# A first batch's weights: W1 fetched in fp32 and cast by ScalarE, with z and W2 moved in GpSimd's order

## The chip, the cores and the metric

The kernel runs on one core of a Trainium2 chip. A core has a matrix engine (TensorE, PE in the profile, with its weight loads as PEld), a vector engine (VectorE, DVE), an activation engine (ScalarE, ACT), GpSimd (POOL) and SyncE (SP), which here only issues DMAs. The engines share an on-chip memory, SBUF, of 128 partitions; TensorE writes into PSUM, from where DVE and ACT read. Engines run on their own and wait for each other by semaphores. DMAs are issued by SP, ACT or POOL and carried out by 16 DMA engines.

The metric is the device time of one execution in microseconds.

## What is computed

For each of 8 batches of 3008 rows: a gated attention without a softmax, and then a feed-forward layer with a quick gelu.

```python
scores = (1 / S) * z @ z.T                  # z: 3008 x 64, S = 3008
attn   = max(scores, 0) ** 2
x      = u * (attn @ v)                     # u, v: 3008 x 256
h      = x @ w_in                           # w_in (W1): 256 x 2048
out    = (h * sigmoid(1.702 * h)) @ w_out   # w_out (W2): 2048 x 256
```

Inputs and output are fp32. The kernel computes in fp16 with fp32 sums in PSUM.

## The kernel before

A batch's 3008 columns of the score matrix are cut into 6 chunks `i` of 512 (the last has 448), its rows into 24 blocks of 128. For chunk `i` the function `attend` gives a list of 47 steps `n` (slots 0 to 46): each multiplies blocks of V by the squared scores of one row block and adds into two PSUM banks. A place in the program is written (i, n) here.

Everything is in one order written out by hand (`manual_schedule`): each engine takes its instructions in the order in which the program names them. The main loop (lines 648 to 714) goes over batches, chunks and slots, and at each slot does in this order what the tables say: `turn_u` (a transpose of u by DVE), `load_u`, `load_w`, `load_z`, `take` (the next scores), an up group, and the step itself.

- `take` (line 613, tables `SCHED0` and others) issues scores ahead of their use. `scores` (line 223) writes a tile of two PSUM banks, of which there are two (`ps2`, `bufs=2`), shared with the up groups. `square` (line 242) lets ACT take the relu (line 256) and DVE square it (line 270). In chunk 3 of batch 0 scores are taken at slots 0, 4, 8, 12, 16, 19, 24 (two), 29, 33, 37, 41 and 45.
- Since the scores are symmetric, half of the squared tiles are gained by transposing others (`turn_unit`, line 293), as DMAs of SP (tiles `tt`).
- `up_group` (line 389) is the first feed-forward product: four matmuls with W1 into a `ps2` tile, the gelu by ACT (line 407), and a scaling to fp16 by DVE (line 411). Sixteen of a batch's 48 run between the steps of chunk 4, which is where W1 is first read. `product` (line 499) is the second, with W2 and four sums of W2's quarters (`weight_sums`, line 442, called in chunk 5), in Strassen's way with seven products.
- In chunks 2, 3 and 5 of batch 0 the steps run on halves of the array: `post` (line 84) puts a `pool.nop` (line 86) into POOL's order after step 23, which waits for the step's matmuls; the first matmul of step 24 waits for it (`behind`, line 91).
- POOL issues most loads: `load_u` (line 188, four DMAs), `load_w` (line 430) and `load_z` (line 152), with a dtype cast from fp32 to fp16 in W's and z's DMAs. `load_z` issues one half of the next batch's z, copies it on POOL once it has landed (line 162), hands it to SP to be transposed into `ZT` (line 163), and does the same with the other half. The two fp16 halves lie in tiles `zst` of tag `y` of the pool `pw`, which has two buffers. The same tag holds the first batch's z in fp32 (`zf`) at the start, and the output tiles `y` later.
- In the first batch the table `LOADW` (line 598) puts W1's four fourths at (3, 16), (3, 24), (3, 32), (3, 40) and W2's at (4, 16), (4, 22), (4, 28), (4, 34). Before the first of them POOL makes a small copy `hold` (line 434) that waits for chunk 1's gated result. `load_z` of the next batch stands at (4, 2) in every batch, and `load_u` of chunk 5 at (4, 8).

Of the kernel before, what the change touches and what calls it, by code (L numbers as in the profile page):

```python
# [9 lines left out]
F32 = mybir.dt.float32  # L10
F16 = mybir.dt.float16
P = 128
# [3 lines left out]
def kernel(  # L16
# [13 lines left out]
    AF = mybir.ActivationFunctionType  # L30
# [4 lines left out]
    DFF = moe_w_in.shape[1]  # L35
# [5 lines left out]
    NCH = (S + CH - 1) // CH  # L41
    CB = CH // P
    NU = NJ // 2
    NCC = D // P
# [11 lines left out]
    dve, act, pe, sp, pool = nc.vector, nc.scalar, nc.tensor, nc.sync, nc.gpsimd  # L56

    const = ctx.enter_context(tc.tile_pool(name="const", bufs=1))
    W1 = const.tile([P, NCC, DFF], F16, name="W1")
# [6 lines left out]
    pw = ctx.enter_context(tc.tile_pool(name="pw", bufs=2))  # L66
# [7 lines left out]
    nil = pw.tile([P, CH], F16, name="nil", tag="gf")  # L74
    dve.memset(nil, 0.0)

    ZP = {}
    late, LATE = [], []
    ZT, V16, UQ, UT, XT, unit, TT = {}, {}, {}, {}, {}, {}, {}

# [40 lines left out]
    def first_cast(g, by_act=False):  # L121
        m = g % CB * CB
        for c in range(2):
            dst, src = ZT["st"][g // CB][:, m:m + CB, c, :], ZT["f"][g // CB][:, m:m + CB, :]
            if by_act:
                act.activation(dst, src, AF.Copy, scale=1.0)  # L126
            else:
                dve.tensor_copy(dst, src)

    def first_zt(g):  # L130

        z2 = ZT["st"][g // CB][:, g % CB * CB:(g % CB + 1) * CB]
        zp = ZP[g] if g in ZP else ps1.tile([P, CB, P], F16, name="zp", tag="ps1")
        for k in range(CB):
            pe.transpose(zp[:, k, :], z2[:, k, :, :], ident)  # L135

        def copies():
            zt = ZT[0][:, g * CB:(g + 1) * CB, :].rearrange("d n p -> d (n p)")
            nb = CB if g < NCH - 1 else CB - 1
            dst = zt[:, :nb * P].rearrange("d (p n) -> d p n", n=nb)  # L140
            src = zp[:, :nb, :].rearrange("d n p -> d p n")
            if g in (0, 2, 3):
                act.activation(dst, src, AF.Copy, scale=1.0)  # L143
            else:
                dve.tensor_copy(dst, src)
            if nb < CB:
                dve.tensor_copy(zt[:, nb * P:], zp[:, nb, :])

        return copies
# [35 lines left out]
    def width(i):  # L185
        return CH if i < NCH - 1 else LAST

    def load_u(b, i):
        eng = pool if b or i else sp
        n = width(i)  # L190
        uq = pu.tile([P, CH // QW, QW, NCC], F32, name="uq", tag="uq")
        src = u[b, i * CH:i * CH + n].rearrange("(q t) c -> t q c", t=QW)
        for k in range(P // QW):
            cs = slice(k * NCC * QW, (k + 1) * NCC * QW)
            eng.dma_start(uq[k * QW:(k + 1) * QW, :n // QW].rearrange("t q c k -> t q (c k)"), src[:, :, cs])  # L195
        UQ[b, i] = uq

    def turn_u(b, i):
        n = width(i)
        ut = pu.tile([P, NCC, CH // QW, QW], F32, name="ut", tag="ut")  # L200
        UT[b, i] = ut
        dve.transpose(  # L202
            ut[:, :, :n // QW, :].rearrange("p k q t -> p q k t"),
            UQ.pop((b, i))[:, :n // QW].rearrange("p q c k -> p q k c"),
        )
# [114 lines left out]
    def full(b):  # L320

        return NCH - 2 if b < B - 1 else NCH - 1
# [107 lines left out]
    def load_w(k):  # L430

        if k == 0:
            hold = const.tile([P, 1], F16, name="hold")
            pool.tensor_copy(hold, XT[0, 1][:, 0, :1])
        if k < 4:
            fs = slice(k * DFF // 4, (k + 1) * DFF // 4)
            pool.dma_start(W1[:, :, fs], moe_w_in.rearrange("(p k) f -> p k f", k=NCC)[:, :, fs])
        else:
            fs = slice((k - 4) * CB, (k - 3) * CB)
            pool.dma_start(W2[:, fs], moe_w_out.rearrange("(fo p) c -> p fo c", p=P)[:, fs])  # L440

    def weight_sums():
        b11, b12, b21, b22 = W2[:, LO, C0], W2[:, LO, C1], W2[:, HI, C0], W2[:, HI, C1]
        t1, t2, t3, t4n = (WT[:, m] for m in range(4))
        return [
            lambda: dve.tensor_tensor(t1, b12, b11, ALU.subtract),  # L446
            lambda: dve.tensor_tensor(t2, b22, t1, ALU.subtract),  # L447
            lambda: dve.tensor_tensor(t3, b22, b12, ALU.subtract),
            lambda: dve.tensor_tensor(t4n, b21, t2, ALU.subtract),
        ]  # L450
# [27 lines left out]
    def products(b):  # L478

        lst = []  # L480
        for k in range(NCH):
            one = [(k, "P6"), (k, "P5"), (k, "P7"), (k, "P2")]
            if blocks(b)[k][1] < CH:
                one.insert(0, (k, "odd"))
            lst += [(k, "P1")] + ([(k - 1, "P4"), (k - 1, "P3")] if k else []) + one
        return lst + [(k, "P4"), (k, "P3")]
# [108 lines left out]
    TURN0 = {(i, (38, 28)[i] if i < 2 else NJ + 4 if i < NCH - 1 else 12): i for i in range(NCH)}  # L595
    LOAD0 = {(1, 14): 2, (2, 12): 3, (2, NJ + 20): 4, (4, 8): 5}
    TURN = {(1, NJ + 4): 2, (2, NJ + 4): 3, (4, NJ + 4): 4, (5, 8): 5}
    LOADW = {(3, 16): 0, (3, 24): 1, (3, 32): 2, (3, 40): 3, (4, 16): 4, (4, 22): 5, (4, 28): 6, (4, 34): 7}
    LOAD = {(3, NJ + 20): 4, (4, NJ + 5): 5}

    FIRST_ZT, FIRST_CAST = {12: 4, 20: 5}, {5: 4, 13: 5}
# [11 lines left out]
    def take(b, n):  # L613
        for post_ in scores(b, [queue.pop(0) for _ in range(n)]):
            post_()

    def fill(b):
        assert not queue
        queue.extend(u_ for i in range(NCH) for u_ in pieces(b, i))
# [24 lines left out]
    copies()  # L644
    ZP[3] = ps1.tile([P, CB, P], F16, name="zp", tag="ps1")
    load_u(0, 1)

    for b in range(B):
        nup = NCH * NFG
        more = b + 1 < B  # L650
        sched = SCHED0 if b == 0 else SCHED if more else SCHED_LAST
        turn, load = (TURN, LOAD) if b else (TURN0, LOAD0)
        head = 0
        for i in range(NCH):
            host = b + 1 if more and i == NCH - 1 else b
            if host > b:
                fill(host)
                LATE.append(host)
            for n, step in enumerate(attend(b, i, b == 0 and i < 2)):
                if b == 0 and i == 0 and n == 5:  # L660
                    load_u(0, 0)
                if b == 0 and i == 0 and n == 2:
                    copies = first_zt(3)
                if b == 0 and i == 0 and n == 3:
                    copies()
                if b == 0 and i == 0 and n in FIRST_CAST:
                    first_cast(FIRST_CAST[n], True)
                if b == 0 and i == 0 and n in FIRST_ZT:
                    first_zt(FIRST_ZT[n])()
                if (i, n) in turn:  # L670
                    turn_u(b, turn[i, n])
                if (i, n) in load:
                    load_u(b, load[i, n])
                if b == 0 and (i, n) in LOADW:
                    load_w(LOADW[i, n])
                if more and (i, n) == (NCH - 2, 2):
                    load_z(b + 1)
                if (b, i, n) == (0, NCH - 1, NJ + 4):
                    for sum_ in weight_sums():
                        sum_()  # L680
                take(host, sched[i].get(n, 0))
                if i == full(b) and n >= HEAD and (n - HEAD) * LAGY // (2 * NJ - 10) >= head and head < LAGY:
                    up_group(b, head)
                    head += 1
                step()
        late.sort(key=lambda t: t[0])
        if more:
            for i in range(2):
                load_u(b + 1, i)
            for n0 in range(0, NJ, VB):  # L690
                load_v(b + 1, n0)
        prods = products(b)
        for q in range(head, nup):
            if more and q in (head + 14, head + 20):
                k = int(q == head + 20)
                turn_u(b + 1, k)
                load_u(b + 1, k + 2)
            up_group(b, q)
            product(b, *prods.pop(0))
            if q >= 30 and q % 2 and late:  # L700
                late.pop(0)[1]()
        steps = [lambda kp=kp: product(b, *kp) for kp in prods]
        for step in steps:
            step()
            for sum_ in [SUMS.pop(0) for _ in range(min(len(SUMS), 1 + (len(SUMS) > 4)))]:
                sum_()
            for _, turn_it in [late.pop(0) for _ in range(min(len(late), 1 + (len(steps) < 10)))]:
                turn_it()
        LATE.clear()
        if more:  # L710
            while late:
                late.pop(0)[1]()
            take(b + 1, 2)
# [30 lines left out]
```

## Time and profile before

| what | value |
|---|---|
| median of 4 runs | 1185.6 us (1185.09 to 1190.59) |
| time of the profiled execution | 1185.6 us |
| its span, first to last instruction | 1183.8 us |
| TensorE busy | 1177.9 us |
| VectorE, ScalarE, GpSimd busy | 841.0, 819.8, 227.4 us |
| granted TensorE clock | 1.0 |
| first batch, to the first step of batch 1 | 161.3 us |
| batch 1, batch 2 | 147.1, 144.2 us |

The page lists each engine's busy time, the chain of work that ended last, and groups of instructions by line. A row of a group has the line, the engine, the operation, what it writes and reads, the count, the busy time, the mean time of one, and the idle time before it with what ended it. The timeline view gives, for one stretch, start, duration, engine, line and count of neighbouring instructions of the same kind, with the engine's idle time before them in brackets. A busy TensorE isn't one at its peak: matmuls overlap, so a hold-up of TensorE is better read from starts than from busy time.

### The profile page before, as it was taken

Reading aid. Unit: us, or ns where it says so; the run is one execution under the profiler, and the core shown is the slowest. Engines: PE = TensorE matmul, PEld = TensorE weight load, DVE = VectorE, ACT = ScalarE, POOL = GpSimd, SP = SyncE. Lnnn points to the kernel's source line nnn. Section 1 sums busy time; section 2 is a strip of 40 time slices with the busy share of each in tenths; the row PEclk is TensorE's granted clock in tenths of the full one; section 3 lists DMA queues with packets and bytes.
Section 4 is the critical chain, followed back from the end, with each engine's and each line's share of the span. In section 5 each row is a group of like instructions: output and inputs, shape, how many; then the busy total and the mean of one; then the engine's idle time right before and its main releaser. Section 6 shows DMA issues by size and latency. Waiting matters only on the chain.

```text
span 1183.8 us, 27920 instructions
## 1 busy us (share of the span) xinstructions
PE 1177.9 (99%) x11526; PEld 699.2 (59%) x11526; DVE 841.0 (71%) x1441; ACT 819.8 (69%) x997; POOL 227.4 (19%) x319
## 2 busy tenths in 40 slices
PE   9999999999999999999999999999999999999998
PEld 3446764467644676447754478545775447844577
DVE  6788865877658776587775877658786587764876
ACT  7878864688646887478764787657866478672785
POOL 5243101231012310133101431014200241001000
PEclk9999999999999999999999999999999999999999
DMA  9997667866777677855779457895659855694012
GB/s 227 184 121 130 134 138 139 80 108 135 143 135 82 108 153 147 128 80 95 157 145 134 77 94 153 162 114 92 111 124 174 110 92 111 131 170 96 1 37 73
DMA packets 378880, 142.88 MB, mean 121 GB/s; under 512 B 320032, under 2 KB 372640, under 8 KB 378752
## 3 DMA queue, kind: packets, MB, share of 16 engines
q1 hardware_dynamic: 320464, 99.39, 45.7%
q0 software_dynamic: 56768, 40.39, 23.1%
q8 instruction: 90, 1.47, 0.5%
q10 hardware_dynamic: 1520, 1.31, 0.3%
q14 instruction: 38, 0.31, 0.1%
HBM read 60.29 MB, written 24.64 MB: 72 GB/s over the span
## 4 chain that ended last, share of the span: by engine, by line
PE 98%; ACT 1%; DVE 1%; issue 0%; DVEq 0%; ACTq 0%; POOLq 0%
PE o L358 40%; PE hg L399 27%; PE st L518 24%; PE sc L235 6%; PE yp L493 1%; ACT rl L256 1%; PE w L99 0%; DVE a L270 0%; ACT ZT L143 0%; DVE ut L202 0%; ACT gf L407 0%; DVE WT L446 0%; DVE WT L447 0%; PE zp L135 0%; ACT zst L126 0%
## 5 line engine op out<-in xcount | busy, mean ns | idle before, releaser
L407 ACT ACTIVATE gf<-hg 128x1024 f32<-128x1024 f32 (+1 forms) x384 | 385.9, 1005 | 146.8 <-PE hg L399 123.3
L256 ACT ACTIVATE rl<-sc 128x1024 f16<-128x1024 f32 (+1 forms) x301 | 287.7, 993 | 146.6 <-PE sc L235 101.4
L358 PEld LDWEIGHTS <-V 64*128 64x128 f16 (+1 forms) x4052 | 217.3, 94 | 254.4 <-issue 11.5
L399 PE MATMUL hg<-xt,W 128*128 128x512 f16 (+1 forms) x1408 | 354.6, 374 | 0.0
L411 DVE TENSOR_SCALAR gt<-gf 128x1024 f16<-128x1024 f32 (+1 forms) x320 | 225.6, 705 | 131.9 <-ACT gf L407 129.0
L358 PE MATMUL o<-a,V 64*128 64x512 f16 (+3 forms) x2240 | 296.0, 368 | 0.0
L270 DVE TENSOR_TENSOR a<-rl 128x1024 f16<-128x1024 f16 (+1 forms) x266 | 177.9, 672 | 116.6 <-ACT rl L256 115.4
L195 POOL DMA_DIRECT2D uq<-in_u_dram x188 | 128.1, 689 | 687.6 <-PE sc L235 445.2
L358 PE MATMUL o<-tt,V 64*128 64x512 f16 (+1 forms) x1510 | 232.1, 377 | 0.1
L399 PEld LDWEIGHTS <-W 128*128 128x128 f16 x1536 | 139.3, 98 | 119.4 <-issue 2.9
L518 PEld LDWEIGHTS <-gt 128*128 128x128 f16 x2944 | 177.1, 98 | 32.2
L518 PEld LDWEIGHTS <-s 128*128 128x128 f16 x2208 | 133.7, 98 | 25.6 <-issue 0.4
L235 PE MATMUL sc<-ZT 64*128 64x512 f16 (+3 forms) x688 | 115.0, 357 | 0.4 <-ACT ZT L143 0.3
L518 PE MATMUL st<-WT,gt 128*128 128x128 f16 x1472 | 97.8, 219 | 0.0
L518 PE MATMUL st<-WT,s 128*128 128x128 f16 x1472 | 96.5, 219 | 0.2 <-ACT uP L530 0.2
L518 PE MATMUL st<-W,gt 128*128 128x128 f16 x1472 | 96.5, 219 | 0.0
L536 DVE SCALAR_TENSOR_TENSOR y<-st,uP 128x256 f32<-128x256 f32 (+1 forms) x144 | 57.8, 408 | 28.5 <-ACT uP L530 20.0
L530 ACT ACTIVATE uP<-st 128x256 f32<-128x256 f32 (+1 forms) x144 | 53.0, 368 | 31.7 <-DVE y L536 15.6
L375 DVE TENSOR_TENSOR xt<-o,ut 128x512 f16<-128x512 f32 x80 | 51.4, 684 | 32.9 <-PE o L358 32.9
L409 ACT ACTIVATE gt<-gf 128x1024 f16<-128x1024 f32 (+1 forms) x64 | 66.0, 1031 | 2.1
L474 DVE TENSOR_TENSOR s<-s,gt 128x1024 f16<-128x1024 f16 (+1 forms) x96 | 64.4, 671 | 1.1
L472 DVE TENSOR_TENSOR s<-gt 128x1024 f16<-128x1024 f16 (+1 forms) x96 | 64.8, 675 | 0.0
(53 smaller groups left out, 602.2 us busy)
## 6 DMA issues: line engine op xcount, KB each, us to landing
out_dram<-y SPq DMA_DIRECT2D x40, 512.0 KB, 3.6
uq<-in_u_dram POOLq DMA_DIRECT2D x156, 128.0 KB, 3.7
V<-in_v_dram POOLq DMA_DIRECT2D x35, 256.0 KB, 6.6
tt<-a SPq DMA_TRANSPOSE x232, 3.8
uq<-in_u_dram POOLq DMA_DIRECT2D x32, 112.0 KB, 4.7
out_dram<-y SPq DMA_DIRECT2D x7, 384.0 KB, 3.0
vst<-in_v_dram SPq DMA_DIRECT2D x3, 512.0 KB, 5.7
zst<-in_z_dram POOLq DMA_DIRECT2D x7, 192.0 KB, 9.0
```

Of the source, the lines that this page charges most:

```text
L195: eng.dma_start(uq[k * QW:(k + 1) * QW, :n // QW].rearrange("t q c k -> t q (c k)"), src[:, :, cs])
L235: pe.matmul(sc[:, r, :q1 - q0], zt[h, 2 * kp + r, :], zt[h].rearrange("d n p -> d (n p)")[:, q0:q1], start=True, stop=True,)
L256: act.activation(rl[:, :, :n], sc[:, :, :n], AF.Relu, scale=csc)
L270: dve.tensor_tensor(a[:, :, :n], rl[:, :, :n], rl[:, :, :n], ALU.mult)
L358: ins = pe.matmul(acc[c][:, :n], V16[b][h, j].rearrange("p (c k) -> p k c", k=NCC)[:, c], weights(b, i, j)[h], start=(k, m) == first[c], s ...
L399: pe.matmul(hg[:, e, :n], W1[:, c, ff * P:(ff + 1) * P], XT[b, i][:, c, :n], start=(c == 0), stop=(c == NCC - 1),)
L407: act.activation(gf[:, :, :n], hg[:, :, :n], AF.Gelu_apprx_sigmoid, scale=1.0 / FSC)
L409: act.activation(g, gf[:, :, :n], AF.Copy, scale=FSC)
L411: dve.tensor_scalar(g, gf[:, :, :n], FSC, None, ALU.mult)
L472: dve.tensor_tensor(s_, a21, a22, ALU.add)
L474: dve.tensor_tensor(s_, ST[b, k, "S1", h], a11, ALU.subtract)
L518: pe.matmul(bank[:, m, :], lhs()[:, f, m, :], right[:, ff, :], start=name in ("P1", "P2", "P5") and m == 0 and ff == 0, stop=ff == NFF // ...
```

## The change

W1's fourths are no longer cast by their DMAs. Each is loaded in fp32 into a tile `wst` of tag `y` (two buffers, shared with `zf` before and `zst` after), and a new function `cast_w` lets ACT cast it into W1. The loads stand at (2, 16), (2, 30), (3, 9), (3, 21), the casts at (3, 8), (3, 20), (3, 42), (4, 6). A slot's cast stands ahead of its loads and its scores. In the first batch `load_z` moves from (4, 2) to (4, 8), where `load_u` of chunk 5 stands ahead of it. W2's loads move to (4, 28), (4, 34), (4, 40) and (5, 0). Later batches are untouched.

```diff
-    ZP = {}
+    ZP, WS = {}, {}
@@ load_w
         if k < 4:
-            fs = slice(k * DFF // 4, (k + 1) * DFF // 4)
-            pool.dma_start(W1[:, :, fs], moe_w_in.rearrange("(p k) f -> p k f", k=NCC)[:, :, fs])
+            WS[k] = pw.tile([P, NCC, DFF // 4], F32, name="wst", tag="y")
+            pool.dma_start(WS[k], moe_w_in.rearrange("(p k) f -> p k f", k=NCC)[:, :, k * DFF // 4:(k + 1) * DFF // 4])
         else:
             fs = slice((k - 4) * CB, (k - 3) * CB)
             pool.dma_start(W2[:, fs], moe_w_out.rearrange("(fo p) c -> p fo c", p=P)[:, fs])
+
+    def cast_w(k):
+        act.activation(W1[:, :, k * DFF // 4:(k + 1) * DFF // 4], WS.pop(k), AF.Copy, scale=1.0)
@@ tables
-    LOADW = {(3, 16): 0, (3, 24): 1, (3, 32): 2, (3, 40): 3, (4, 16): 4, (4, 22): 5, (4, 28): 6, (4, 34): 7}
+    LOADW = {
+        (2, 16): 0, (2, 30): 1, (3, 9): 2, (3, 21): 3, (4, 28): 4, (4, 34): 5, (4, 40): 6, (5, 0): 7,
+    }
+    CASTW = {(3, 8): 0, (3, 20): 1, (3, 42): 2, (4, 6): 3}
@@ main loop
+                if b == 0 and (i, n) in CASTW:
+                    cast_w(CASTW[i, n])
                 if b == 0 and (i, n) in LOADW:
                     load_w(LOADW[i, n])
-                if more and (i, n) == (NCH - 2, 2):
+                if more and (i, n) == (NCH - 2, 2 if b else 8):
                     load_z(b + 1)
```

## The prediction

> **What bounds the kernel now.** I read the page's engine totals and its chain first, then TensorE's own waits in the first batch, then the timelines of ScalarE (ACT), TensorE (PE) and GpSimd (POOL) in the stretch that the change touches, 34 to 96 us.
>
> ```profile
> span 1183.8 us, 27920 instructions
> PE 1177.9 (99%) x11526; PEld 699.2 (59%) x11526; DVE 841.0 (71%) x1441; ACT 819.8 (69%) x997; POOL 227.4 (19%) x319
> PE 98%; ACT 1%; DVE 1%; issue 0%; DVEq 0%; ACTq 0%; POOLq 0%
> ```
>
> TensorE is busy in 1177.9 of 1183.8 us and carries 98% of the chain. The list of TensorE's waits between 40 and 160 us has one entry:
>
> ```profile
> PE st L518 <- ACT uP L530: 0.2, 1, 0.2
> ```
>
> So the loads that the change moves cost TensorE nothing that can be seen today: no wait on W1, W2 or z stands there. What can be won is that 0.2 us and perhaps some tenths of short hesitations. What can be lost is any time for which something new holds TensorE, since it has no idle time to pay from.
>
> The stretches' busy time for chunk 3 (columns: length, then PE, PEld, DVE, ACT, POOL, then clock, DMA share, GB/s), and ACT's timeline; the 13th of the first row's relus and the ones in slots 4 and 8 are shown again by themselves, from narrow windows:
>
> ```profile
> 50.20:62.70 12.50, 12.50 (x122) 5.83 (x118) 10.35 (x19) 11.63 (x14) 4.53 (x7) 1.00 1.26 168
> 44.10 12.44 ACT L256 ACTIVATE rl<-sc 128x1024 f16<-128x1024 f32 x13 [2.00 <-PE sc L235]
> 51.60 1.02 ACT L256 ACTIVATE rl<-sc 128x1024 f16<-128x1024 f32 x1
> 52.73 1.02 ACT L256 ACTIVATE rl<-sc 128x1024 f16<-128x1024 f32 x1
> 55.62 0.92 ACT L256 ACTIVATE rl<-sc 128x896 f16<-128x896 f32 x1
> 56.89 5.53 ACT L256 ACTIVATE rl<-sc 128x896 f16<-128x896 f32 x6 [0.35 <-PE sc L235]
> 62.96 1.28 ACT L407 ACT_TABLE_LOAD   x1
> 64.28 1.02 ACT L407 ACTIVATE gf<-hg 128x1024 f32<-128x1024 f32 x1
> 65.79 1.02 ACT L407 ACTIVATE gf<-hg 128x1024 f32<-128x1024 f32 x1 [0.49 <-PE hg L399]
> ```
>
> ACT works 11.63 of 12.50 us there: 0.87 us are free. The change puts three casts into just this stretch. TensorE's scores in it, with the steps between, and POOL's queue:
>
> ```profile
> 54.39 0.35 PE L235 MATMUL sc<-ZT 64*128 64x448 f16 x2
> 55.23 0.35 PE L235 MATMUL sc<-ZT 64*128 64x448 f16 x2
> 56.49 0.54 PE L235 MATMUL sc<-ZT 64*128 64x448 f16 x4
> 56.87 1.24 PE L358 MATMUL o<-a,V 64*128 64x512 f16 x10
> ...
> 57.26 2.10 POOL L437 DMA_DIRECT2D W<-in_moe_w_in_dram  x3 [5.65 <-PE sc L235]
> 59.36 1.02 POOL L158 DMA_DIRECT2D zst<-in_z_dram  x1
> 70.85 0.83 POOL L162 COPY zst<-zst 128x768 f16<-128x768 f16 x1 [10.47 <-DMA zst<-in_z_dram]
> 71.62 1.25 POOL L158 DMA_DIRECT2D zst<-in_z_dram  x1
> 79.63 0.89 POOL L162 COPY zst<-zst 128x768 f16<-128x768 f16 x1 [5.62 <-DMA zst<-in_z_dram]
> 83.16 4.00 POOL L440 DMA_DIRECT2D W<-in_moe_w_out_dram  x4
> L437 POOL DMA_DIRECT2D W<-in_moe_w_in_dram x4: 700/707/716, 50.9 to 58.7; - x4
> DMA to landing us min/median/max: 5.7/8.4/9.7
> ```
>
> The scores at 54.39, 55.23 and 56.49 (two tiles) are chunk 3's slots 16, 19 and 24; slots 8 and 12 stand at 52.26 and 53.34, slot 29 at 57.95. The `o` matmul at 56.87 is step 24, which waits for the POOL signal of line 86. That signal stands at the end of step 23 in POOL's order; today POOL is idle before it, and fires as soon as step 23 is done.
>
> **The change, part by part.** The time of the profiled run is 1185.6, its span 1183.8; 1.8 lies around it, and the median of the four runs is the same 1185.6. I add to 1185.6.
>
> *W1 out of its old slots, into (2,16), (2,30), (3,9), (3,21).* Four DMAs of 0.7 us of POOL each, as before. The small copy `hold` and the first DMA now run about 39 us, when chunk 1's gate is done, the second after chunk 2's signal at 44. Cast 0 and cast 1 want them at 52.6 and 57: 13 us each, against landings of 5.7 to 9.7. Cost 0. The DMA share in this stretch is already over 1 (1.26 in chunk 3), so the transposes of SP will land later; but those issued at 37 to 51 are first read in steps at 54.6 (slot 16) and after 64, some 10 us behind their landing, and that is their cover. If it went, the first loser would be chunk 3's step 16.
>
> *Cast 0 (slot 8).* The nearest row is ACT's copy with a scale of 128x1024 f32 to f16, 1057 ns on line 409; relus and gelus of that size take 1.02, and I take 1.03. It follows the relu of 51.60, which ends at 52.62, and ends at 53.65. The relu of slot 8 begins at 53.65 instead of 52.73 and ends at 54.67. Scores have two PSUM tiles, so slot 16's scores at 54.39 wait for it: 0.3 us.
>
> *Cast 1 (slot 20) and the third and fourth loads.* Behind slot 8 ACT runs without a gap at 0.92 a relu (5.53 us for six): slot 12 to 55.59, 16 to 56.51, 19 to 57.43, cast 1 to 58.46. The second tile of slot 24's scores waits for slot 19's relu. Load 3 takes cast 1's buffer (two buffers of tag y), so POOL waits at (3,21) till 58.46, and behind that wait in POOL's queue stands step 23's signal; who waits for the signal is TensorE. Today it goes from signal (56.70) to matmul (56.87) in 0.17, so step 24 begins at about 58.7 instead of 56.87: 1.8 us, the 0.3 above included. If neighbouring ACT instructions overlap by 0.1, as a pitch under the duration would give, it is 1.3; if the signal must also wait for the DMA's 0.7 on POOL, 2.5. I take 1.6, nearer to the middle of the first two, since rows show POOL's sequencer running ahead of an executing DMA (line 158's semaphore instruction of 58.1 lies inside the DMAs of 57.26 to 59.36). Load 2 at (3,9) waits for cast 0 too, but nothing is late for it.
>
> Whether the signal stands behind the wait at all is where trace and notes differ. POOL's copy waited till 70.85 for z, and the semaphore instruction of the next z load, behind it in program order, also ran only at 70.8: the sequencer stood still at the wait. The Trainium skill, PSUM — Partial Sum Buffer, "Engine vs sequencer instructions", has a sequencer go on once earlier instructions are dispatched; read loosely, the signal would pass the waiting load and this term would fall to what ACT alone forces. The row decides, and the sum goes by it.
>
> ACT alone would force 0.9 to 1.3 in that case: slot 29's scores (57.95) need slot 24's first relu, which ends 0.92 after cast 1, at 58.8 (with the overlap) to 59.4.
>
> *Casts 2 (slot 42) and 3 (chunk 4, slot 6).* Cast 2 comes behind slot 41's relu, about 64, and pushes the last relu, the table load (1.28) and the first gelu by 1.0; today there is 0.49 idle before the second gelu. The third up group then waits for the first gelu: 0.2. Cast 3 goes between second and third gelu, and the gelus' pitch of 1.3 to 1.5 against 1.02 takes it up: 0. Bounds 0 and 0.5. The loads were issued when cast 0 and cast 1 ended, 53.7 and 58.5, and are wanted at about 64 and 68.5: a cover of 10 us against landings of 5.7 to 9.7 for 256 KB written, and now 512 KB are written. z's 192 KB took 11.4 (59.36 to 70.8). Bounds 0 and 2 (1 each at 11.4, rounded up); I take 0, as most rows (u's pieces at 5.3 to 7.2, v's 512 KB at 4.9 to 7.2) lie below 10.
>
> *z at (4,8), W2 at (4,28) to (5,0).* u's load 5 stands before z in POOL's order now. z's first load can start when cast 2 has freed its buffer, near 65 instead of 59.4, but without W1 beside it. By 7.5 us a load (the second z load) the copies end near 74 and 83, by 11.4 near 77 and 89; today 71.7 and 80.5. The first half of ZT is wanted at 87.4, the second at 96, and a transpose takes 5.7; SP's next item behind z's second one is the `ad` transpose at 90.5. Then W2's four loads, 4.0 of POOL, which wait for nothing: slots late in chunk 4 are passed while POOL still waits for z, so they start at 83 to 89, and not later for their new slots. They land by 93 to 99.5; line 447 wants the last of them at 96.0 plus the shift, line 86's signal of chunk 5 stands behind them at 92.5 plus the shift. Cost 0, at most 1.7.
>
> Sum: 1.6 + 0.2 = 1.8, so 1187.4. The ends: 0 (or 0.5 won) and 2.5 + 0.5 + 2 + 1.7 = 6.7.
>
> **The rivals.**
> *Nothing is lost.* The signal passes the wait, ACT's overlap and its 0.87 of slack take most of the rest. For it: relus are already issued closer than their length. Against: 3.1 us of casts into 0.87. 1185.6 to 1186.2.
> *A gain.* Without W1 beside them z and the late transposes land sooner. For it: transposes of 8 to 10 us there, a DMA share of 1.26. Against: TensorE waits for none of them. At most 0.5: 1185.1.
> *Slower by over 0.5%.* Load 3 lands late and ACT, which takes its work in order, stands at cast 3 with the gelus behind it. Place: chunk 4, about 68.5. Price: 1 us for each us of landing past 10. It decides from 1191.5, so from a landing of about 14 us; no row shows one. For it: twice the bytes, DMA share over 1. About 1193.
> *z and W2 late.* Both z loads at 11.4: 1.7 more, 1189.1.
> *The change does not do what it says* in one respect: W2 and z are where POOL's waits put them, whatever their slots. That is in the sum already.
>
> **How the numbers follow.** Likeliest 0.60 (1187.4, its own range 1186.4 to 1188.6); nothing lost 0.18; gain 0.04; z and W2 late 0.10; load 3 late by over 4 us 0.08. What a measurement of this kernel can tell from no change is about 0.5%, 5.9 us: all but the last case and a rest of 0.01 lie inside. Faster 0.01, same 0.91, slower 0.08. The range 1185.2 to 1190.6 leaves out the tail of the late loads and half of the gain, and so under 2 in 10.
>
> **What would show it.** Right: four ACT casts of about 1.03 us near 52.6, 57.5, 64 and 69; TensorE's waits between 40 and 160 us get an entry of 1 to 2 us at line 358 released by POOL's line 86, with step 24 near 58.5; batch 1 begins near 163 instead of 161.3 and every later batch keeps its length. Wrong: step 24 on time with ACT's relus late (the signal passed), a long ACT wait on a DMA before a cast, or waits of line 447 or line 235 for W2 or ZT in chunk 5.

## The result and the profile after

The changed kernel takes 1186.85 us in the median of 54 executions, against 1185.58 for the kernel before: 1.27 us more. The ratio of the means is 1.0023, with a 95% interval of 1.0013 to 1.0033, which is 2.7 us; it is larger than the medians' difference because single executions of the changed kernel, 11 of 54, take 1191 us and more, and 3 of 77 of the kernel before do. The longest one, 1211.85, stands outside that ratio as a slow one, and three executions of over 1350 us (one each of the experiments e4 and e7 and of the kernel before) are left out of the counts below. So there are two results to explain: a loss of about 1.3 us in the ordinary executions (1.38 between the lowest of the two kernels, 1.27 between the medians), and a tail, as the long executions of a kernel are called here.

The page and the list of TensorE's waits between 40 and 160 us, of the changed kernel:

```profile
span 1184.6 us, 27928 instructions
PE 1177.3 (99%) x11526; PEld 699.2 (59%) x11526; DVE 840.5 (71%) x1441; ACT 822.4 (69%) x1001; POOL 225.5 (19%) x319
PE o L358 <- POOLq L86: 0.9, 1, 0.9
PE st L521 <- ACT uP L533: 0.2, 1, 0.2
```

ACT has four instructions and 2.6 us more, and a new wait stands in TensorE's list: step 24 of a half-array chunk, held by POOL's signal of line 86. The timelines of the changed kernel show the chain behind it, first ACT's (line 443 is the new cast), then POOL's, then TensorE's:

```profile
52.15 1.05 ACT L443 ACTIVATE W<-wst 128x1024 f16<-128x1024 f32 x1
53.09 3.44 ACT L256 ACTIVATE rl<-sc 128x1024 f16<-128x1024 f32 x4
56.39 1.09 ACT L443 ACTIVATE W<-wst 128x1024 f16<-128x1024 f32 x1
57.33 1.75 ACT L256 ACTIVATE rl<-sc 128x896 f16<-128x896 f32 x2
...
63.28 1.05 ACT L443 ACTIVATE W<-wst 128x1024 f16<-128x1024 f32 x1
...
67.85 1.06 ACT L443 ACTIVATE W<-wst 128x1024 f16<-128x1024 f32 x1
```

```profile
38.74 0.72 POOL L437 DMA_DIRECT2D wst<-in_moe_w_in_dram  x1 [0.34 <-issue]
44.24 0.71 POOL L437 DMA_DIRECT2D wst<-in_moe_w_in_dram  x1 [4.78 <-PE sc L235]
...
53.49 0.72 POOL L437 DMA_DIRECT2D wst<-in_moe_w_in_dram  x1 [3.05 <-ACT W L443]
57.77 0.71 POOL L437 DMA_DIRECT2D wst<-in_moe_w_in_dram  x1 [3.56 <-ACT W L443]
...
64.62 1.03 POOL L158 DMA_DIRECT2D zst<-in_z_dram  x1 [0.89 <-ACT W L443]
71.19 0.96 POOL L162 COPY zst<-zst 128x768 f16<-128x768 f16 x1 [5.54 <-DMA zst<-in_z_dram]
...
80.85 3.23 POOL L440 DMA_DIRECT2D W<-in_moe_w_out_dram  x4
```

```profile
54.16 0.37 PE L235 MATMUL sc<-ZT 64*128 64x448 f16 x2
...
56.26 0.69 PE L235 MATMUL sc<-ZT 64*128 64x448 f16 x4
57.83 1.26 PE L358 MATMUL o<-a,V 64*128 64x512 f16 x10 [0.88 <-POOLq L86]
...
67.10 1.02 PE L399 MATMUL hg<-xt,W 128*128 128x512 f16 x4
```

TensorE's first steps of chunk 3, of the kernel before and of the changed one:

```profile
50.31 0.81 PE L358 MATMUL o<-a,V 64*128 64x512 f16 x6
49.94 1.03 PE L358 MATMUL o<-a,V 64*128 64x512 f16 x8
```

Cast 1 ends at 57.48 (56.39 + 1.09). POOL's fourth load was waiting for it and starts at 57.77; the signal behind it in POOL's order comes in the same moment, at 57.8; step 24 begins at 57.83. This execution is 0.37 us ahead of the one before when chunk 3 begins (49.94 against 50.31); scores at 29.70 and 30.08 have the same difference, ahead of anything that the change moves, so it belongs to the execution and not to the change. Step 24 is thus 57.83 - 56.87 + 0.37 = 1.33 us late. The third up group is at 67.10 instead of 66.02: 1.45 late. Chunk 5 begins at 87.92 instead of 87.01, 1.28 late: at 84.1 the kernel before hesitates for 0.17 at an up group, and the changed one no longer does. Batch 1 keeps its length within about 0.1 (it begins at 162.18 and 161.27, batch 2 at 309.40 and 308.37). 1.28 agrees with the medians' 1.27, more closely than two single executions could be trusted to.

### The profile page after: what moved, and what is told of

It is laid out like the page before. It is cut to its first block, busy times and chain, and to the rows that moved or that the text cites. A ratio compares the mean times of both kernels' runs of the same rounds, so it can differ in the third digit from the quotient of the medians.

```text
span 1184.6 us, 27928 instructions
## 1 busy us (share of the span) xinstructions
PE 1177.3 (99%) x11526; PEld 699.2 (59%) x11526; DVE 840.5 (71%) x1441; ACT 822.4 (69%) x1001; POOL 225.5 (19%) x319
## 4 chain that ended last, share of the span: by engine, by line
PE 97%; issue 1%; ACT 1%; DVE 1%; POOL 0%; DVEq 0%; POOLq 0%; ACTq 0%
PE o L358 39%; PE hg L399 27%; PE st L521 24%; PE sc L235 5%; ACT rl L256 1%; PE yp L496 1%; PE w L99 0%; DVE ut L202 0%; POOL uq L195 0%; ACT ZT L143 0%; DVE a L270 0%; ACT gf L407 0%; DVE WT L449 0%; DVE WT L450 0%; POOL wst L437 0%
## 5 line engine op out<-in xcount | busy, mean ns | idle before, releaser
L539 DVE SCALAR_TENSOR_TENSOR y<-st,uP 128x256 f32<-128x256 f32 (+1 forms) x144 | 57.8, 408 | 28.5 <-ACT uP L533 20.0
```

## Experiments

Each was timed beside the kernel before on the same chip, whose median lay between 1185.41 and 1185.56. The counts of long executions are gathered here, for those runs that were timed more than once.

| kernel | executions | lowest | median | over 1188 | over 1191 |
|---|---|---|---|---|---|
| before, with the changed kernel's runs | 77 | 1184.96 | 1185.58 | 14 | 3 |
| before, beside the three groups of experiments | 97 | 1184.88 | 1185.41 to 1185.55 | 11 | 2 |
| changed, first runs and again | 65 | 1186.26 | 1186.85, 1186.84 | 17 | 13 |
| e1, fourth load behind the signal | 12 | 1185.81 | 1186.42 | 5 | 2 |
| e4, casts only | 10 | 1185.99 | 1186.32 | 1 | 0 |
| e7, one load, four casts | 10 | 1185.91 | 1186.07 | 0 | 0 |
| e3, all loads early, fp32 | 12 | 1185.77 | 1188.27 | 7 | 4 |
| e2, z and W2 only | 11 | 1185.16 | 1187.03 | 4 | 1 |
| e5 and e11, early loads, cast by DMA | 22 | 1184.61 | 1185.51, 1185.27 | 0 | 0 |
| e9, the change's slots, cast by DMA | 12 | 1184.95 | 1185.42 | 2 | 1 |
| e8, two more fp32 loads | 12 | 1185.47 | 1192.46 | 9 | 8 |
| e10, two more loads into fp16 | 12 | 1184.77 | 1185.51 | 3 | 3 |

### What the loss in the ordinary executions is made of

**e1: the fourth load behind the signal.**

```diff
-        (2, 16): 0, (2, 30): 1, (3, 9): 2, (3, 21): 3, ...
+        (2, 16): 0, (2, 30): 1, (3, 9): 2, (3, 24): 3, ...
```

> The changed kernel with W1's fourth load at (3, 24) instead of (3, 21), so that it stands behind chunk 3's signal in POOL's order and nothing else moves. Theory (the signal stands behind the load's wait for cast 1): step 24 no longer waits for line 86; slot 29's scores then wait some 0.5 us for ACT instead; some 0.8 to 0.9 us stay of the changed kernel's 1.3 over the kernel before, so about 1186.4. Rival (ACT's own load makes the whole loss): the same time as the changed kernel, 1186.85. Second rival (the signal was the whole loss): the time of before, 1185.6. For the few executions of the changed kernel that take 1190 to 1203 us: if the late landing of the fourth load makes them, they stay as frequent here.

Measured: median 1186.42 (ratio 1.0018, 1.0007 to 1.0028), lowest 1185.81 against the changed kernel's 1186.26. Step 24 no longer waits for line 86; slot 29's scores wait for ACT, by TensorE's timeline:

```profile
56.88 1.26 PE L358 MATMUL o<-a,V 64*128 64x512 f16 x10
58.45 0.36 PE L235 MATMUL sc<-ZT 64*128 64x448 f16 x2 [0.31 <-ACT rl L256]
```

With chunk 3 beginning at 50.05 here, slot 29's scores are 58.45 - 57.95 + 0.26 = 0.76 late. So the signal is worth 0.6 us of the 1.33 by the timelines and 0.35 to 0.45 by the times, and ACT the rest. The profile is of an execution of 1191.1 us and is read again below.

**e4: the casts alone.**

```diff
+    def cast_x(k):
+        src = UT[0, 2 + k // 2].rearrange("p k q t -> p (k q t)").rearrange("p (f c) -> p f c", c=P)
+        act.activation(WT[:, k], src, AF.Copy, scale=1.0)
+    CASTX = {(3, 8): 0, (3, 20): 1, (3, 42): 2, (4, 6): 3}
+                if b == 0 and (i, n) in CASTX:
+                    cast_x(CASTX[i, n])
```

> The kernel before with four ACT copies of 128x1024 f32 to f16 added at the changed kernel's cast slots, from tiles of u into a tile that is written again later; no load moved. Theory: ACT's time alone costs 0.8 to 0.9 us: 1186.4. Rival (ACT's slack and overlap take them): 1185.6 to 1185.8. The executions above 1192: none, since no ACT instruction here waits on a DMA's landing.

Measured: median 1186.32, 0.8 above the kernel before beside it. The ratio of the means, 1.0005 (0.9996 to 1.0014), doesn't tell it from the kernel before, whose mean holds its own long executions (6 of 35 over 1188); the lowest times do, 1185.99 against 1184.91. The same 0.31 us wait at slot 29's scores stands in its list of TensorE's waits:

```profile
PE sc L235 <- ACT rl L256: 0.3, 1, 0.3
```

Slot 29's scores stand at 58.66 and chunk 3 begins at 50.27, so they are 0.75 late, as in e1. This is agreement from two sides: ACT's time in chunk 3, with no load moved at all, is some 0.8 us, and the held signal the rest.

**e7: one load, four casts.**

```diff
+        if 0 < k < 4:
+            return
-        act.activation(W1[...], WS.pop(k), AF.Copy, scale=1.0)
+        act.activation(W1[...], WS[0], AF.Copy, scale=1.0)
```

> The changed kernel with W1's loads 1 to 3 left out: all four casts read the first fourth, so W1 holds one fourth four times and the output is another one. Casts, z and W2 stand where the changed kernel has them; POOL waits for no cast. Theory: ACT's 0.8 stays, 1186.0 to 1186.4, and with 1.5 MB less of traffic the transposes keep up: TensorE waits for no tt, and no execution stands above 1192. Rival (the casts make the tail): tail as in the changed kernel.

Measured: median 1186.07, 0.5 above before, highest 1187.08; the ratio of the means is 0.9999 (0.9990 to 1.0009). Its profiled execution took 4406.86 us, so only the times are used, and that TensorE waits for no `tt` here is not shown. No tail in these 10 executions, as the theory has it. That the loss is 0.5 here and 0.8 in e4 isn't explained by a trace; between the lowest executions it is 1.03 here and 1.08 in e4, so the medians' difference may be scatter.

### What the tail is

**e1 and e12 caught long executions in profile.** e1's, of 1191.1 us: TensorE's waits between 40 and 160 us, ACT's timeline, and the landing of the third load, issued at 53.60:

```profile
PE o L358 <- DMA tt<-a: 2.9, 2, 1.7
PE hg L399 <- ACT gf L407: 0.9, 1, 0.9
PE hg L399 <- ACT rl L251: 0.7, 1, 0.7
PE sc L235 <- ACT rl L256: 0.3, 1, 0.3
```

```profile
64.63 1.06 ACT L443 ACTIVATE W<-wst 128x1024 f16<-128x1024 f32 x1 [1.71 <-DMA wst<-in_moe_w_in_dram]
```

```profile
DMA to landing us min/median/max: 11.0/11.0/11.0
```

Two things hold TensorE. The larger is `tt`, the transposed tiles that SP's DMAs make: chunk 4 waits for them at its slots 16 and 20. The smaller is a cast that waits for its load: the third took 11.0 us, ACT stood for 1.71, and two up groups were held behind it. The changed kernel in a short execution shows neither; its loads took 5.2 to 8.1.

```profile
DMA to landing us min/median/max: 5.2/6.4/8.1
```

**e8 and e12: two more loads on the kernel before.**

```diff
+    def more_w(k):
+        more_ = pw.tile([P, NCC, DFF // 4], F32, name="wst", tag="y")
+        pool.dma_start(more_, moe_w_in.rearrange("(p k) f -> p k f", k=NCC)[:, :, k * DFF // 4:(k + 1) * DFF // 4])
+    MOREW = {(2, 16): 0, (2, 30): 1}
+                if b == 0 and (i, n) in MOREW:
+                    more_w(MOREW[i, n])
```

> The kernel before with two more fp32 loads of a fourth of W1 each at (2, 16) and (2, 30) into tiles of tag y that nothing reads; its own loads of W1 stay. Theory: the fastest executions as before, 1185.2 to 1185.7, but a longer tail than the kernel before has on the same chip, with executions above 1192, and in a profile of a slow one waits of line 358 for tt. Rival (traffic is hidden by the transposes' lead): the same times as before, tail too.

> The run with two more fp32 loads, looked at once more for a profile of a slower execution. Theory: if it takes over 1189, TensorE's waits show line 358 held by tt in chunk 4 for about the excess, or line 399 held by a gelu, and SP issues its last transposes of the first batch after 66 us.

Measured: e8 has a median of 1192.46 (ratio 1.0053, 1.0028 to 1.0077), 8 of 12 over 1191, up to 1203.59, while its lowest is 1185.47. No cast, no wait for a cast and no moved load is in it: 1 MB of traffic by itself makes a tail, and a worse one than the change's (W1's own loads still run here too, from 50.9 to 59 us). e12, the same kernel, took 1188.94, just under the 1189 that was named; as expected, its TensorE timeline has the excess in chunk 4 at slots 12, 16 and 20:

```profile
70.23 0.61 PE L358 MATMUL o<-tt,V 128*128 128x512 f16 x2 [0.73 <-DMA tt<-a]
...
72.31 0.39 PE L358 MATMUL o<-tt,V 128*128 128x512 f16 x1 [0.18 <-DMA tt<-a]
...
77.21 0.38 PE L358 MATMUL o<-tt,V 128*128 128x512 f16 x1 [2.14 <-DMA tt<-a]
```

The last transpose of line 298 in the first batch tells how near an execution is to this. From SP's rows for that one DMA alone, issue (first start) and time to landing, of the kernel before, the changed one, the changed one again, and e12:

```profile
L298 SPq DMA_TRANSPOSE tt<-a x1: 2972/2972/2972, 57.3 to 57.3; - x1
DMA to landing us min/median/max: 10.0/10.0/10.0
```

```profile
L298 SPq DMA_TRANSPOSE tt<-a x1: 2877/2877/2877, 64.5 to 64.5; - x1
DMA to landing us min/median/max: 7.0/7.0/7.0
```

```profile
L298 SPq DMA_TRANSPOSE tt<-a x1: 3347/3347/3347, 64.7 to 64.7; - x1
DMA to landing us min/median/max: 9.5/9.5/9.5
```

```profile
L298 SPq DMA_TRANSPOSE tt<-a x1: 1284/1284/1284, 71.5 to 71.5; - x1
DMA to landing us min/median/max: 5.7/5.7/5.7
```

They land at 67.3, 71.5, 74.2 and 77.2; slot 20 of chunk 4 was due at 74.0, 75.1 and 75.2 in the first three. The lead is 6.7 us before, 3.6 and 1.0 in two short executions of the changed kernel, and gone in e12 and e1 (67.9 + 11.7 = 79.6, and slot 20 at 79.70). SP issues its transposes one after the other, and the last one's issue moves from 57 to 64, 68 and 71 us. The longest single issue of line 298 after 37 us grows too: 3.6 us before, 3.8 and 5.8 in the changed kernel, 5.4 in e12 and 7.4 in e1. That SP is held there by earlier transposes that haven't landed is inferred.

**e3: all loads early, no wait for a cast.**

```diff
-            WS[k] = pw.tile([P, NCC, DFF // 4], F32, name="wst", tag="y")
+            WS[k] = pw.tile([P, NCC, DFF // 4], F32, name="wst", tag="gf" if k < 2 else "y")
-        (2, 16): 0, (2, 30): 1, (3, 9): 2, (3, 21): 3, ...
+        (2, 16): 0, (2, 18): 1, (2, 30): 2, (2, 32): 3, ...
```

> The changed kernel with W1's loads at (2, 16), (2, 18), (2, 30), (2, 32), the first two into tiles of tag gf, the others into tag y, so that no load waits for a cast; casts, z and W2 as in the changed kernel. Theory: the signal of chunk 3 comes on time, ACT's 0.8 to 0.9 us stay: 1186.4. With every fourth landed by about 55 us, no ACT wait on a DMA is left: if late landings of the third and fourth load make the executions of 1190 to 1203 us, none are seen here. Rival for those: they come from elsewhere (z, W2, or u's load ahead of them) and stay.

Measured: 1188.27, 7 of 12 over 1188 and 4 over 1191. A miss: I had expected the tail to go. In the profiled execution (1188.49) no cast waits for a load, and the tail's other part is there, a `tt` wait of 1.1 us at slot 16. TensorE's waits between 40 and 160 us, ACT's timeline, and VectorE's (DVE's) waits between 40 and 85 us:

```profile
PE o L358 <- DMA tt<-a: 1.1, 1, 1.1
PE hg L399 <- ACT gf L407: 0.9, 1, 0.9
PE hg L399 <- ACT rl L251: 0.4, 1, 0.4
65.19 0.49 ACT L251 ACTIVATE rl<-sc 128x384 f16<-128x384 f32 x1 [1.21 <-DVE a L270]
DVE a L270 <- DMA tt<-a: 2.9, 2, 2.4
```

The transposes hold TensorE on a second way here: DVE can't write its next square `a` until a transpose has read the old one (2.9 us of waiting), ACT's last relu waits 1.21 for DVE, and two up groups wait for ACT. So the waits at line 399 that in e1 come from a late load come from the transposes here. Late loads are thus not needed for the tail. That it comes more often the more traffic lies in this stretch fits e3 and e8 and isn't tested by itself.

**e6: the changed kernel again.**

> The changed kernel as it is, on the same chip as its companions here. All theories: the fastest executions near 1186.4. The tail theory above: 2 or 3 of some 12 above 1191.

Measured: 1186.84, two of 11 over 1191 (1195.98 and 1205.3).

**e5 and e11: the early slots, but cast by the DMA.**

```diff
-    LOADW = {(3, 16): 0, (3, 24): 1, (3, 32): 2, (3, 40): 3, (4, 16): 4, ...
+    LOADW = {(2, 16): 0, (2, 30): 1, (3, 9): 2, (3, 21): 3, (4, 16): 4, ...
```

> The kernel before with W1's four loads at the changed kernel's slots, (2, 16), (2, 30), (3, 9), (3, 21), but cast by their DMAs as before, with no ACT cast and no wait for one; z and W2 as before. Theory (loads between 39 and 57 us slow SP's transposes, which fall behind in their queue until chunk 4's steps wait for them in some executions): the fastest executions as before, 1185.2 to 1185.6, and a tail over 1192 as in the changed kernel, in 1 to 3 of some 12. Rival (the tail comes from ACT's casts waiting for a landing): no execution above 1192.

> The kernel before with W1's loads at the changed kernel's slots and cast by their DMAs, once more. If moving these loads ahead shortens the tail that the kernel before has of its own (single executions of 1187 to 1192): again none above 1187 here, and some in the runs of the kernel before beside it. If it was luck: 2 or 3 of some 12 between 1187 and 1192.

Measured: 1185.51 and 1185.27, highest of 22 executions 1187.03. e5's expectation failed: the early slots make no tail. By itself that fits e5's rival, that the casts' waits make it; e8, which has no cast, and e3, where no cast waits, speak against the rival as the whole. e5's last `tt` is issued as late as the changed kernel's, at 64.2, but lands in 3.3 us, at 67.5, a lead as before. Of the kernel before, 25 of 174 executions lie over 1188, of these 22 none; that is a weak hint that the early slots are better for its own tail, as by that share three would be expected, and as beside e11 the kernel before had none in 28 either.

**e9: all of the change's slots, cast by the DMA.**

```diff
-    LOADW = {(3, 16): 0, (3, 24): 1, (3, 32): 2, (3, 40): 3, (4, 16): 4, (4, 22): 5, (4, 28): 6, (4, 34): 7}
+    LOADW = {(2, 16): 0, (2, 30): 1, (3, 9): 2, (3, 21): 3, (4, 28): 4, (4, 34): 5, (4, 40): 6, (5, 0): 7}
-                if more and (i, n) == (NCH - 2, 2):
+                if more and (i, n) == (NCH - 2, 2 if b else 8):
```

> The changed kernel's slots for W1, z and W2 on the kernel before, with W1 cast by its DMAs: the change without its fp32 and without ACT's casts. Theory (the median's loss is ACT's casts and the held signal, the tail is the transposes behind the fp32 traffic): 1185.5, and no execution above 1192. Rival (early slots make the tail, and the 11 executions of the run with early loads were lucky): 2 or 3 of some 12 above 1191.

Measured: 1185.42 (ratio 1.0004, 0.9992 to 1.0015), with single executions of 1188.27 and 1192.0. The change without fp32 and casts is the kernel before in its median, so all of the median's loss is in the fp32 form, not in the slots. For the tail, one of 12 executions over 1191 against 13 of 65 is too few to tell alone; with e5 and e11 it is one of 34, which points to the fp32 form, though those two leave z and W2 where they were.

**e2: z and W2 alone.**

```diff
-    LOADW = {..., (4, 16): 4, (4, 22): 5, (4, 28): 6, (4, 34): 7}
+    LOADW = {..., (4, 28): 4, (4, 34): 5, (4, 40): 6, (5, 0): 7}
-                if more and (i, n) == (NCH - 2, 2):
+                if more and (i, n) == (NCH - 2, 2 if b else 8):
```

> The kernel before with only z moved to (4, 8) and W2's loads to their new slots; W1 as before, cast by its DMAs. Theory (POOL passes these slots while it waits for z, and all of it is covered): 1185.6, no difference, and no executions above 1192. Rival (z and W2 late in some executions): the same median, but single executions of 1194 to 1203 as in the changed kernel.

Measured: lowest 1185.16, but median 1187.03 and 4 of 11 over 1188 (ratio 1.0016, 1.0006 to 1.0027). A miss. The profiled execution is a short one (1185.63) without a new wait, but its last `tt` is issued at 59.7 and takes 12.6 us, so it lands 1.6 before slot 20. POOL now issues u's load 5 at 60.67, ahead of z, right behind W1's three loads at 57.21 and beside the last transposes; before, it was issued at 80.47. That this is the cause is argued from the rows, not shown; with W1 early as well (e9) the same places cost nothing in the median.

**e10: the two more loads, into fp16.**

```diff
-        more_ = pw.tile([P, NCC, DFF // 4], F32, name="wst", tag="y")
+        more_ = pw.tile([P, NCC, DFF // 4], F16, name="wst", tag="y")
```

> The run with two more loads at (2, 16) and (2, 30), but with fp16 tiles, cast by the DMA, so that each writes 256 KB instead of 512. Theory (it is the bytes written that hold up the transposes): a tail much smaller than with fp32 tiles, the median under 1187. Rival (the reads or the number of packets count): the same tail as with fp32 tiles, a median over 1190.

Measured: median 1185.51, 3 of 12 between 1193 and 1197, against 8 of 12 over 1191 with fp32. Halving the bytes written while the reads stay as they are makes the tail rarer (3 of 12 over 1188 against 9 of 12), and does not end it. The two were timed apart; beside them the kernel before had 0 of 28 and 5 of 34 over 1188.

**What stays open.** The long executions that were profiled are the shorter ones, of 1188.49, 1188.94 and 1191.1 us; there TensorE's waits listed above make up the excess to within 0.5 us (4.5 of 4.7 in e1 and 2.4 of 2.1 in e3, over 1186.4; 3.0 of 3.4 in e12, over 1185.5). Longer ones were only timed. Their granted clock is lower: it is 0.999 or 1.0 in every execution up to 1190 us for which it is on record, and 0.991 to 0.998 in 25 of the 34 over 1191. By estimate, 0.4% of 1203 us is 4.8 us of the 16 by which the changed kernel's execution of 1203.07 (clock 0.996) exceeds its median. Whether TensorE's waits bring the lower clock, or the clock has another cause, was not tested; e1's executions of 1191.1 and 1192.11 are long at a clock of 1.0, so the clock is not needed for a long one.

## Why the prediction was right, and where it was not

The time, 1186.85, is in the range and 0.55 below the forecast of 1187.4, and "same" (0.91) is what came. The signs named for it came too: four casts, at 52.15, 56.39, 63.28 and 67.85, and a wait of line 358 on line 86, of 0.9 where 1 to 2 was said. Step by step:

- *Cast 0, slot 16's scores, 0.3:* 0.14 (54.16 against 54.39 less 0.37).
- *Cast 1 and the signal, 1.6 with ends 1.3 and 2.5:* 1.33. The mechanism is the one told, TensorE held by line 86 behind a load that waits for a cast. The size was off because neighbouring ACT instructions overlap: the relu after cast 0 starts 0.94 after it, though the cast takes 1.05. The 5.53 us for six relus was misread as a pitch of 0.92: the first two start 0.81 apart (56.89 and 57.70), the last three 1.05 apart, which is the pace of the scores. So cast 1 ended 0.61 before the 58.46 of the sum (57.48 + 0.37 = 57.85). Step 24 then came 0.35 after that end and not 0.24, which took some of it back. The low end was the right one, partly by these two errors against each other, and I had taken the middle. The 0.7 of the load's own time is not in it: the signal came with the load's start.
- *The signal stands behind the wait:* right, with the load at 57.77 and the signal at 57.8. The loose reading of the Trainium skill (PSUM — Partial Sum Buffer, "Engine vs sequencer instructions") by which it would pass a waiting load does not hold for this signal and this load; what passes a running DMA is a semaphore instruction, and only once the DMA's own wait is over.
- *ACT alone, 0.9 to 1.3:* 0.8 in e4 and 0.9 in e1 by medians, 0.75 and 0.76 at slot 29's scores, so the low end or just under it.
- *Casts 2 and 3, 0.2:* 0.12 (1.45 less 1.33).
- *z and W2, 0:* right in the profile: z's copies at 71.2 and 79.8, W2 from 80.85, no wait for either. e9 agrees, with W1 early; with W1 in its old slots (e2) the same move costs 1.5 in the median.
- *Not in the sum:* the 0.17 at 84.1 that went away, one of the "short hesitations" that were named as a possible gain. e4's execution, which moves no load, lacks it too (up groups at 83.71 and 85.01), so the moved loads need not be the reason. 1.33 + 0.12 - 0.17 = 1.28.

The step that failed is one that I put at 0 for the wrong reason. "... so the transposes of SP will land later; but those issued at 37 to 51 are first read ... some 10 us behind their landing, and that is their cover." Two more are issued after 51, the last at 57.3, landing at 67.3 and read at slot 20 at 74.0: the cover was 6.7, not 10. I also took each DMA's delay by itself, but SP issues its transposes one after the other, and the last one's issue moved (57.3 before, 64.5 in the changed kernel, 71.5 in e12). And the place of the first loss is not chunk 3's step 16 but chunk 4's slots 12, 16 and 20. In the median the cover held; one execution of five is long (13 of 65 over 1191). These lie above the range's end, 1190.6; what the range leaves out there was put down to late loads alone. The rival "slower by over 0.5%" had another mechanism, a cast that waits for its load; e1 shows that too (11.0 us of landing, 1.71 of wait for ACT, at cast 2 instead of cast 3), but as the smaller part. No profile of the changed kernel itself in a long execution was caught; that its tail is the same as that of e1, e3 and e12 is inferred from e9, e5 and e11, which have one execution of 34 over 1191 without the fp32 form.

## What to carry to other kernels

Where one engine is busy all the time, an edit elsewhere can win little and cost much, and the price is read from what the moved instruction waits for and what stands behind it in its queue: a load that waited for a buffer held the signal that its engine gives after it. Before extra bytes go into a stretch where the DMA engines are full, look up the last transfer of the longest queue there, not a typical one, and how far ahead of its reader it lands. Compare several executions, not one: the changed kernel had a lead of 1 to 4 us and no wait for `tt` in two profiled executions, and took over 10 us more in others.

## What the runs showed of the hardware

- A cast inside a DMA was the better bargain here: with fp16 written (e9, e5) the early loads cost nothing in the median; with fp32 written and ACT casting the same loads cost 1.3 us in the median, and 13 of 65 executions lie between 1191 and 1212 us.
- When SP's transposes land differs between executions of the same program: in two short executions of the changed kernel the last one landed at 71.5 and at 74.2.
- ACT's neighbouring instructions start closer than their duration: 0.94 after a cast of 1.05, and 1.94 us for two gelus of 1.02 (from 66.02 in the changed kernel).
